# An exponential on VectorE in fewer steps, beside ScalarE's: attention and a Mish layer on one Trainium2 core

## The chip, the cores and the metric

The kernel runs on one core of one Trainium2 chip. The core has five engines that run their own instruction streams and meet at semaphores: TensorE (PE, matrix products into the PSUM banks), ScalarE (ACT), VectorE (DVE), GpSimd (POOL) and SyncE (SP, which here issues most of the DMAs). The metric is the time of one execution on the device in microseconds. The kernel before takes 830.16 us (median of three runs, 829.76 to 830.72).

## The reference, cut to what matters

`x` has 2048 tokens of 640 features in bf16. One branch is full softmax attention with 32 heads of 20 features. The other is a dense layer with 1536 hidden features and the Mish activation. A gate per token mixes the two.

```python
g = sigmoid((x * gate_w).sum(-1, keepdims=True))
qkv = (x @ wqkv).reshape(B, S, 3, 32, 20)            # to q, k, v per head
scores = einsum("bhqd,bhkd->bhqk", q, k) * 20 ** -0.5
a = einsum("bhqk,bhkd->bhqd", softmax(scores), v) ... @ wo
h = x @ w1 + b1
b = (h * tanh(softplus(h))) @ w2
return g * a + (1 - g) * b
```

The scores hold 32 x 2048 x 2048 values, and each needs an exponential. That is the bulk of the elementwise work.

## The kernel before, in words

**Tiling.** A *unit* is one head's scores for 128 keys against 512 queries: one PSUM bank of 128 x 512 floats. There are 2048 units. They are ordered in *groups* `(c, g)`: query block `c` of 512 queries, head group `g` of 4 heads, 16 key tiles. The order is all `g` with `c` = 0 and 1 first, then `c` = 2, then `c` = 3, whose last head group is cut into two halves of 256 queries. Three units make a *slot* (`compose`); there are 683 slots, and two sets of three PSUM banks take turns.

**One slot.** `emit_s` puts the three score products on TensorE (`score_mms`, L1149). Each uses 32 rows of the array, so the three run side by side. `emit_e` (L1171) puts one exponential over the slot on ScalarE, from PSUM to the tile `ETS` in bf16 (five slots deep, `NETS`). `emit_pv` and `pv` (L1456) then multiply V with the exponentials of four heads at a time. Four products side by side make one *pass* that accumulates into the bank `ACC`. V has a column of ones, so the sums of the softmax come out with it. After a group's last pass `group_done` copies the accumulator out (L1537) and divides.

**Units on VectorE.** For some slots `choose` takes a unit out of the order and gives it to VectorE as the third of the slot. Then ScalarE's instruction covers only two units (1024 columns a row instead of 1536). `emit_x` (L1216) evicts the third: scaled and biased, the float becomes an int16 whose bits, read as bf16, are 2^e times a linear mantissa. Four such units make a *batch*. When it is full (or `tight` says that its group ends soon), `close` queues the rest of its work on VectorE:

- `fraction` (L1287): the mantissa bits with the exponent of one, F, into the pad `u`
- `power` (L1283): the exponent bits alone, E, into the pad `E`
- `square` (L1291): F times F, to fp16, in place in `u`
- `cubes` (L1330): V scaled by a constant, into the tile `VC`, once per head group and key tile
- `times_f` (L1295): F squared times the evicted value, in `u`

The exponential is then a sum of three terms, and `emit_off` adds them by three passes on TensorE: the evicted value with V, E with V, and `u` with the scaled V. A *pad* is a tile of four units of bf16. Pads are borrowed from buffers that are not in use at the time (`open_pads`, `take_pad`, `give_pad`): parts of `QT`, `KT`, `OTN`, `HB`, `W2R`, `REG`, `PADS`.

**What sets the order.** The whole program is written out in Python before it runs. `Plan` keeps an estimated clock per engine (constants at the top: `EXP`, `QUAD`, `DOUBLE`, `CHAIN` and others) and puts each instruction where it fits by that clock. On VectorE, `work` picks among lanes: the division of a finished group (`norm`), the batches (`soon`, two lanes), Mish (`blend`) and others (`bg`). On TensorE, dense products (*tasks*: the projections, the hidden layer at L911, its second product at L970, the output at L994) are put into the gaps with due times (`pick`, `put`), and `fill_up` adds repeated or idle products where TensorE would rest too long. Whether a unit goes to VectorE is decided in `choose`, by VectorE's backlog (`BEHIND`, `crowded` with `IDLE`), by the distance to the group's end (`tight` with `CROWD` and `MARGIN`), by free pads, and by `room` for what VectorE still owes.

**The guard.** The bit form of the exponential holds only for a limited range of scores. `gram_task` bounds the scores from products of the weights and of `x` with themselves, `flag_ops` and `flag_end` compare the bound with `SAFE`, and if it is exceeded a second, safe program runs after the first.

Of the kernel before, what the change touches and what calls it, by code (L numbers as in the profile page):

```python
# [8 lines left out]
FP32 = mybir.dt.float32  # L9
BF16 = mybir.dt.bfloat16  # L10
I32 = mybir.dt.int32
I16 = mybir.dt.int16
# [24 lines left out]
NETS = 5  # L37
# [4 lines left out]
SAFE = 30.0  # L42
# [11 lines left out]
SPUN = 0.6  # L54
# [4 lines left out]
HALF_WORK = 0.60  # L59
LANES = 2  # L60
TAKEN = 3.6
LATE_OFF = 0.8
# [4 lines left out]
CHAIN = 4.4  # L67
FILL = 2.5
GIVE_BACK = 30
IDLE = 6  # L70
QUAD = 0.60
DOUBLE = 1.134
CUBES = 0.022
AHEAD = 14
SPREAD = 2
GAP = 0.8
SLOW_LOAD = 5.0
EARLY = 4
BEHIND = 7.0
PATIENCE = 3.0  # L80
CATCH_UP = 5.0
BUSY = 0.6
CROWD = 1.4
MARGIN = 0.5
EAGER = 30
# [6 lines left out]
LAG = 9  # L92
SPARE = 3.5
# [3 lines left out]
PACKED_Q = 12  # L97
# [7 lines left out]
REFILL = 0.58  # L105
# [15 lines left out]
MANTISSA = 0x7F  # L121
EXPONENT = 0x7F80
ONE = 0x3F80
# [110 lines left out]
def bass_gated_mix__softmax_full_mha__dense_activation_mish__prompt_kernel(  # L234
# [39 lines left out]
    VC = sb("VC", [P, NKT, HG, EW], BF16)  # L274
# [7 lines left out]
    MXR = OUTT[:, 48:56].bitcast(FP32)  # L282
    GW = OUTT[:, 64:64 + NFT]
# [93 lines left out]
    def attention(pl, fast):  # L377
# [133 lines left out]
        if fast:  # L511
# [29 lines left out]
            blank = OTN[0:NG, 0, 0:2, :].rearrange("p g t -> p (g t)")[:, 0:D]  # L541
            m_blank = pl.add("dve", lambda e: e.memset(blank, 0.0), cost=0.25)
# [282 lines left out]
            def gram_task(n, due):  # L825
# [3 lines left out]
                blocks = [(WQ, WK)[n] for _ in range(4)] if n < 2 else [WQ, WK] if n == 2 else [xt(n - 3)] * 4  # L829

                def mm(b, f):
                    at = 4 if n == 2 else b
                    block = blocks[b][:, f, at * P:(at + 1) * P]
                    return lambda e, bank: e.matmul(
                        PS[:, bank, b * P:(b + 1) * P], block, block, start=(f == 0), stop=(f == NFT - 1))

                def finish(bank, last):
                    for reads in ([wq_read], [wkv_read], [wq_read, wkv_read])[n] if n < 3 else [x_read[n - 3]]:
                        reads.append(last)
                    if n == 2:  # L840
                        to, src = MXS[:, 1:4:2], PS[:, bank, 0:2 * P].rearrange("p (a b) -> p a b", b=P)
                    else:
                        to, src = MXS[:, (0, 2, 0, 4, 5, 6, 7)[n]:][:, 0:1], PS[:, bank, :]
                    grams[n] = dve(lambda e: e.tensor_reduce(to, src, AX.X, ALU.max), [last], WIDE)
                    if len(grams) == 7:
                        bg.append((0.3, lambda: flag_ops(grams.values()), None))
                    return grams[n]

                return Task([mm(b, f) for b in range(len(blocks)) for f in range(NFT)], 0.06, finish, due,
# [236 lines left out]
        open_batch = [None]  # L1086
        batches = {}
        n_batches = [0]
        cubed = {"of": None, "tiles": set(), "read": None}
# [123 lines left out]
        def emit_x(s):  # L1213
# [8 lines left out]
            if len(batch["units"]) == BATCH:  # L1222
                close()
# [7 lines left out]
        def close():  # L1231
# [763 lines left out]
```

## Time and profile before

| | |
|---|---|
| median of 3 runs | 830.16 us (829.76 to 830.72) |
| the profiled execution's own time | 830.66 us |
| its span, first to last instruction | 828.8 us |
| ScalarE busy | 809.2 us, 98% |
| VectorE busy | 763.7 us, 92% |
| TensorE busy | 745.7 us, 90% |
| exponentials on ScalarE (L1171) | 683 instructions, 790.1 us |
| mean granted TensorE clock | 0.994 |
| DMA | 48.51 MB, 59 GB/s on average |

All times of the trace are of that one execution. "Busy" is the time in which an engine has at least one instruction in flight; instructions of one engine overlap a little, so the recorded durations add up to more. A row of a group gives the line, the engine, the operation, the tiles written and read, the shape, the count, then busy time and the mean duration in ns, and last the idle time ahead of it and what ended it. In a table of stretches, a row gives the window, its length, and for each engine the busy time with the number of instructions in brackets, then the granted clock, the DMA share and GB/s.

### The profile page before, as it was taken

To read this page: it belongs to the slowest core of one execution; us is meant where nothing else is said; L and a number is where in the kernel's file an instruction comes from. 1 tells how busy PE (TensorE), PEld (TensorE's weight loads), DVE (VectorE), ACT (ScalarE), POOL (GpSimd) and SP (SyncE) were. 2 spreads that over 40 slices of the span, in tenths; PEclk is the share of its full clock that TensorE was granted. 3 is DMA by queue.
4 is the path that set the end of the run, shared out by engine and by line. 5 is a ranking of instruction groups with operands and counts; after the bars stand their busy time and mean duration, and the time that the engine had idled before them with its cause. 6 is when DMAs were issued, how large, how long until landed. Compare 5 with 4: busy or idle time off the path is not lost.

```text
span 828.8 us, 16585 instructions
## 1 busy us (share of the span) xinstructions
PE 745.7 (90%) x6839; PEld 267.3 (32%) x6876; DVE 763.7 (92%) x1204; ACT 809.2 (98%) x714; POOL 7.3 (1%) x14
## 2 busy tenths in 40 slices
PE   8998988989888989889998998999889899999996
PEld 3333233233222333223333333333333333333332
DVE  4898878999999999988899899999999999999886
ACT  6999999999999999999999999999999999999995
POOL 3000000000000000000000000000000000000000
PEclk9999999999999999999999999999999999999998
DMA  9712210121123312141121221102121202100001
GB/s 228 94 52 76 66 59 11 50 72 57 47 59 97 113 47 60 54 118 40 37 72 34 59 62 49 50 15 58 58 70 46 78 15 64 51 22 23 23 19 37
DMA packets 78183, 48.51 MB, mean 59 GB/s; under 512 B 23964, under 2 KB 73748, under 8 KB 78052
## 3 DMA queue, kind: packets, MB, share of 16 engines
q1 hardware_dynamic: 75732, 46.87, 21.2%
q8 instruction: 57, 0.93, 0.5%
q10 hardware_dynamic: 2256, 0.47, 0.3%
q0 software_dynamic: 112, 0.01, 0.2%
q14 instruction: 26, 0.21, 0.1%
HBM read 37.64 MB, written 7.52 MB: 54 GB/s over the span
## 4 chain that ended last, share of the span: by engine, by line
ACT 91%; PE 5%; DVE 3%; issue 0%
ACT ETS L1171 88%; ACT REG L944 2%; PE PS L1149 1%; PE PS L1456 1%; ACT W2R L944 1%; PE PS L545 1%; PE PS L590 0%; PE PS L911 0%; PE PS L659 0%; DVE HB L1291 0%; DVE QT L1216 0%; PE PS L730 0%; DVE W2R L1216 0%; PE PS L765 0%; DVE HB L1000 0%
## 5 line engine op out<-in xcount | busy, mean ns | idle before, releaser
L1171 ACT ACTIVATE ETS<-PS 128x1024 bf16<-128x1024 f32 (+1 forms) x683 | 790.1, 1410 | 4.4 <-PE PS L1149 3.4
L1149 PE MATMUL PS<-QT,KT 32*128 32x512 bf16 (+1 forms) x2148 | 271.0, 378 | 66.1 <-ACT ETS L1171 48.4
L1456 PE MATMUL PS<-ETS,V_all 128*21 128x512 bf16 (+1 forms) x1783 | 191.2, 380 | 0.1
L1149 PEld LDWEIGHTS PS<-QT,KT 32*128 32x128 bf16 x2148 | 68.2, 91 | 270.9 <-ACT ETS L1171 234.2
L970 PE MATMUL PS<-W2R,HB 128*128 128x320 bf16 x384 | 72.8, 302 | 0.3 <-DVE XB L977 0.3
L1456 PEld LDWEIGHTS PS<-ETS,V_all 128*21 128x21 bf16 x1783 | 47.5, 90 | 76.6 <-issue 72.6
L1216 DVE TENSOR_SCALAR QT<-PS 128x512 int16<-128x512 f32 x76 | 52.0, 684 | 5.4 <-PE PS L1149 5.2
L911 PE MATMUL PS<-XB,REG 128*128 128x256 bf16 x360 | 55.4, 277 | 0.8 <-DVE HB L921 0.4
L1216 DVE TENSOR_SCALAR OTN<-PS 128x512 int16<-128x512 f32 x71 | 48.3, 680 | 2.0 <-PE PS L1149 1.8
L1216 DVE TENSOR_SCALAR PADS<-PS 128x512 int16<-128x512 f32 x61 | 41.6, 683 | 5.9 <-PE PS L1149 5.7
L970 PEld LDWEIGHTS PS<-W2R,HB 128*128 128x128 bf16 x384 | 29.3, 97 | 36.0 <-issue 26.0
L911 PEld LDWEIGHTS PS<-XB,REG 128*128 128x128 bf16 x360 | 28.9, 98 | 26.6 <-issue 24.1
L921 DVE TENSOR_TENSOR HB<-PS,B1T 128x512 bf16<-128x512 f32 x48 | 32.8, 684 | 3.2 <-PE PS L911 2.7
L1216 DVE TENSOR_SCALAR REG<-PS 128x512 int16<-128x512 f32 x35 | 23.9, 682 | 4.2 <-PE PS L1149 4.1
L1291 DVE TENSOR_TENSOR QT<-QT 128x1024 f16<-128x1024 bf16 (+2 forms) x35 | 25.0, 717 | 0.0
L994 PE MATMUL PS<-WOQ,QT 128*128 128x320 bf16 x128 | 24.3, 302 | 0.6 <-DVE QT L1530 0.5
L792 PE MATMUL PS<-REG,XB 128*128 128x160 bf16 (+1 forms) x240 | 23.4, 234 | 1.3 <-DVE WOQ L668 0.8
L994 PE MATMUL PS<-WOQ,OTN 128*128 128x320 bf16 x128 | 24.0, 302 | 0.1
L1216 DVE TENSOR_SCALAR KT<-PS 128x512 int16<-128x512 f32 x34 | 23.1, 681 | 0.6 <-PE PS L1149 0.6
L1537 DVE COPY OUNG<-PS 128x512 f32<-128x512 f32 x31 | 21.1, 682 | 1.6 <-PE PS L1456 1.4
L659 PE MATMUL PS<-XB,WOQ 128*128 128x512 bf16 x66 | 20.5, 383 | 1.9 <-issue 1.3
L944 ACT ACTIVATE REG<-HB 128x1024 f32<-128x1024 bf16 x18 | 22.2, 1236 | 0.0
(229 smaller groups left out, 900.2 us busy)
## 6 DMA issues: line engine op xcount, KB each, us to landing
REG<-in_B_w_dram SPq DMA_DIRECT2D x36, 320.0 KB, 3.1
BCT<-SUMS SPq DMA_DIRECT2D x124, 64.0 KB, 2.1
W2R<-in_B_w_dram SPq DMA_DIRECT2D x12, 320.0 KB, 3.3
KT<-KS SPq DMA_DIRECT2D x28, 128.0 KB
QT<-QS SPq DMA_DIRECT2D x112, 20.0 KB
QS<-WOQ SPq DMA_DIRECT2D x16, 128.0 KB, 1.7
KS<-OTN SPq DMA_DIRECT2D x16, 128.0 KB, 1.7
W2R<-in_B_w_dram SPq DMA_DIRECT2D x1, 1920.0 KB, 8.5
```

The costliest lines, as they stand in the source:

```text
L792: return lambda e, bank: e.matmul(PS[:, bank, i * n:(i + 1) * n], xt(t // 4)[:, f, t % 4 * P:(t % 4 + 1) * P], WV[:, f, g * HD:g * HD + n] ...
L911: return lambda e, bank: e.matmul(PS[:, bank, i * HW:(i + 1) * HW], w1b(n1)[:, f, i * P:(i + 1) * P], xt(c)[:, f, cols], start=(f == 0), s ...
L921: ev = dve(lambda e: e.tensor_tensor(hb, PS[:, bank, :].rearrange("p (i t) -> p i t", i=2), bias, ALU.add), [last, b_load, *guarded, *b_re ...
L944: ex = pl.add("act", lambda e: e.activation(U, h, AF.Tanh, scale=0.5, bias=-MISH_AT / 2), [ev, u_free[0]], cost=0.95)
L970: return lambda e, bank: e.matmul(PS[:, bank, 0:HALF], HB[:, hc % 2, f, t * P:(t + 1) * P], W2[:, f, half * HALF:(half + 1) * HALF], start ...
L994: return lambda e, bank: e.matmul(PS[:, bank, 0:HALF], otn(c, g, fast)[:, t * P:(t + 1) * P], WOG[:, g, half * HALF:(half + 1) * HALF], st ...
L1149: op = pl.add("pe", lambda e, i=i, g=real(g), tile=tile, j=j, cols=cols, c=c, of_q=of_q: e.matmul(scores(s)[:, i, cols], KT[32 * j:32 * j ...
L1171: e_op[s] = pl.add("act", lambda e: e.activation(ETS[:, s % NETS, 0:n, :], scores(s)[:, 0:n, :], AF.Exp, scale=SCALE, bias=LIFT if fast el ...
L1216: ev = dve_by(lambda e: e.tensor_scalar(block(batch["y"], n, I16), scores(s)[:, 2, :], SCALE * ULPS, BIAS, ALU.mult, ALU.add), [s_op[s], * ...
L1291: return lambda e: e.tensor_tensor(some_of(batch["u"], sp, FP16), some_of(batch["u"], sp, BF16), some_of(batch["u"], sp, BF16), ALU.mult)
L1456: lasts[n] = pl.add("pe", lambda e, v=v, j=j, src=src[:, cols], of_q=of_q, count=count: e.matmul(PS[32 * j:32 * j + EW, ACC, of_q], v, src ...
L1537: ev = dve(lambda e: e.tensor_copy(src, PS[:, ACC, :]), [last, oung_free[0]], WIDE)
```

## The change

The exponential on VectorE gets two terms in place of three. The eviction now makes an int16 whose bits are read as fp16 (10 bits of mantissa, 5 of exponent). `fraction` puts the mantissa under the exponent of one half. The product `times_y` multiplies that with the evicted value itself. `power` keeps the exponent bits, sets one low bit and works in place in the evicted pad. The two pads, read as fp16, are multiplied with the same bf16 V. The square, the scaled V (`VC`) and the third pad are gone. Since fp16 has a smaller range, `SAFE` goes from 30 to 9.75, and the guard bounds the weights by the row sums of absolute values within each head.

Two batches may be open at once. A pass with V is put out when two are ready, or when the oldest waiting unit is three slots old. `ETS` has six slots, and a number of the planner's constants are changed.

```diff
-NETS = 5
+NETS = 6
+OLD = 3
+WAITED = 3
+OWE = 0.6
-SAFE = 30.0
+SAFE = 9.75
-SPUN = 0.6
+SPUN = 0.65
-LATE_OFF = 0.8
+LATE_OFF = 0.5
-CHAIN = 4.4
+CHAIN = 3.3
-IDLE = 6
+IDLE = 5
+IDLE_2 = 4
+IDLE_3 = -1
+OPEN = 2
-GAP = 0.8
+GAP = 0.5
-BEHIND = 7.0
-PATIENCE = 3.0
+BEHIND = 8
+PATIENCE = 5
-CROWD = 1.4
-MARGIN = 0.5
-EAGER = 30
+CROWD = 1.6
+MARGIN = 2.5
+EAGER = 20
-LAG = 9
-SPARE = 3.5
+LAG = 25
+SPARE = 7
-PACKED_Q = 12
+PACKED_Q = 15
-REFILL = 0.58
+REFILL = 0.66
-ULPS = 128 / math.log(2)
-CUBE = 0.1669921875
-BIAS = 16113
-LIFT = (BIAS - 128 * (127 - 1.1157324)) * math.log(2) / 128
+ULPS = 1024 / math.log(2)
+BIAS = 15 * 1024 + 436
+LIFT = math.log(1.5069154) + 436 / ULPS
-MANTISSA = 0x7F
-EXPONENT = 0x7F80
-ONE = 0x3F80
+MANTISSA = 0x3FF
+EXPONENT = 0x7C00
+HALVES = 0x3800
+MORE = 8
...
-    VC = sb("VC", [P, NKT, HG, EW], BF16)
...
+                        got = dve(lambda e: e.tensor_reduce(
+                            sums, PS[0:w, bank, 0:heads * DH].rearrange("p (h d) -> p h d", d=DH), AX.X, ALU.add,
+                            apply_absolute_value=True), [last, m_mxs], WIDE)
...
             def reserve():
                 def run():
                     batch["u"], got["u"] = take_pad(batch)
-                    batch["E"], got["E"] = take_pad(batch)
...
+            def fraction(sp):
+                return lambda e: e.tensor_scalar(
+                    some_of(batch["u"], sp, I16), some_of(y, sp, I16), MANTISSA, HALVES, ALU.bitwise_and, ALU.bitwise_or)
+
+            def times_y(sp):
+                return lambda e: e.tensor_tensor(
+                    some_of(batch["u"], sp, FP16), some_of(batch["u"], sp, FP16), some_of(y, sp, FP16), ALU.mult)
+
             def power(sp):
                 return lambda e: e.tensor_scalar(
-                    some_of(batch["E"], sp, I16), some_of(y, sp, I16), EXPONENT, None, ALU.bitwise_and)
-            def square(sp):
-                return lambda e: e.tensor_tensor(
-                    some_of(batch["u"], sp, FP16), some_of(batch["u"], sp, BF16), some_of(batch["u"], sp, BF16), ALU.mult)
-            def times_f(sp):
-                return lambda e: e.tensor_tensor(
-                    some_of(batch["u"], sp, BF16), some_of(batch["u"], sp, FP16), some_of(y, sp, BF16), ALU.mult)
+                    some_of(y, sp, I16), some_of(y, sp, I16), EXPONENT, MORE, ALU.bitwise_and, ALU.bitwise_or)
...
             piece(QUAD, fraction, lambda: [*evs, *got["u"]], step("f"))
-            piece(QUAD, power, lambda: [*evs, *got["E"]], end_e)
-            piece(DOUBLE, square, lambda: [got["f"]], step("s"), True)
-            cubes()
-            piece(DOUBLE, times_f, lambda: [got["s"]], end, True)
+            piece(DOUBLE, times_y, lambda: [got["f"]], end, True)
+            piece(QUAD, power, lambda: [got["u"]], end_e)
...
             if s - 1 not in off:
                 return False
-            if open_batch[0]:
-                todo += len(open_batch[0]["units"]) * CHAIN / BATCH
+            todo += sum(len(b["units"]) for b in opened) * CHAIN / BATCH
             run = 1 + (s - 2 in off) * (1 + (s - 3 in off))
-            return todo >= (IDLE, IDLE - 2, -1)[run - 1]
+            return todo >= (IDLE, IDLE_2, IDLE_3)[run - 1]
...
+            def fits(group, taken):
+                mine = [v for v in near[2:] if v[:2] == group and v[3] not in taken and v[2] < tiles(*group) - 1]
+                return [v for v in mine if v[2] < 3] if near[2][:2] != group else mine
+
+            for batch in list(opened):
+                group = batch["group"]
+                mine = fits(group, js + [u[3] for u in batch["units"]])
+                if mine and len(batch["units"]) < BATCH:
+                    break
+                if not mine and near[2][:2] != group and place[near[2][:2]] > place[group]:
+                    close(batch)
+            else:
+                if len(opened) == OPEN:
+                    return None
                 group = near[2][:2]
...
-                if not free_pads() or len(open_pads()) - waiting - 1 < 2 or tiles(*group) < 4:
+                if not free_pads() or len(open_pads()) - waiting - 1 < 1 or tiles(*group) < 4:
...
-                for name in ("F", "E", "U"):
+                for name in ("U", "E"):
...
-                    home = batch[{"F": "y", "E": "E", "U": "u"}[name]]
-                    deps = batch["evs"] if name == "F" else [op]
-                    lasts = pv([(u, block(home, i), deps if i == 0 else []) for i, u in enumerate(batch["units"])], name == "U")
+                    home = batch["u" if name == "U" else "y"]
+                    lasts = pv([(u, block(home, i, FP16), [op] if i == 0 else []) for i, u in enumerate(batch["units"])])
...
-                emit_off((c, g), False, False, 1)
+                if passes > 50 or pl.now["pe"] + PASS + (SWITCH if pl.kind != "V" else 0) <= latest[0]:
+                    emit_off((c, g), False, False, 1)
...
-                if passes < 50 and queue[0][0] > step - 2 and pl.now["pe"] + PASS + (SWITCH if pl.kind != "V" else 0) > latest[0]:
+                if passes < 50 and queue[0][0] > step - OLD and pl.now["pe"] + PASS + (SWITCH if pl.kind != "V" else 0) > latest[0]:
...
-            emit_pv(step, 2 if step < NSLOT - 1 else 99)
-
-            while owed > 0:
+            turn = not fast or step >= NSLOT - 1 or pv_ready() >= 2 or bool(queue) and queue[0][0] <= step - WAITED
+            if turn:
+                emit_pv(step, 2 if step < NSLOT - 1 else 99)
+
+            while owed > (OWE if turn and fast and step < NSLOT else 0):
```

More of the change, by code (lines that the diff above doesn't have):

```diff
@@ L541, in attention @@
             blank = OTN[0:NG, 0, 0:2, :].rearrange("p g t -> p (g t)")[:, 0:D]
+            m_mxs = pl.add("dve", lambda e: e.memset(MXS, 0.0), cost=0.1)
             m_blank = pl.add("dve", lambda e: e.memset(blank, 0.0), cost=0.25)
@@ L1240, in close @@
             evs = list(batch["evs"])
-            batch["parts"]["F"] = evs[-1]
             got = {}
@@ L1298, in end @@
             def end(op):
-                batch["parts"]["U"] = op
-                batch["read"].append(op)
+                got["u"] = batch["parts"]["U"] = op
             def end_e(op):
                 batch["parts"]["E"] = op
-            def cubes():
-                of = real(group[1])
-                need = sorted({tile for u in batch["units"] for tile, _, _ in subs(*u[:3])})
-                def wait():
-                    if any((of, tile) not in v_done for tile in need):
-                        return False
-                    if cubed["of"] == of:
-                        return None
-                    if any("U" not in b["begun"] for at in groups[:place[group]] for b in batches.get(at, ())):
-                        return False
-                    return cubed["read"]
-                def run():
-                    deps = []
-                    if cubed["of"] != of:
-                        deps.append(cubed["read"])
-                        cubed.update(of=of, tiles=set())
-                    if all(tile in cubed["tiles"] for tile in need):
-                        return
-                    t0, t1 = min(tile for tile in range(NKT) if tile not in cubed["tiles"]), need[-1] + 1
-                    while t1 < NKT and (of, t1) in v_done and safe(v_done[(of, t1)]) <= pl.now["dve"]:
-                        t1 += 1
-                    cubed["tiles"].update(range(t0, t1))
-                    pl.add("dve", lambda e: e.tensor_scalar(
-                        VC[:, t0:t1, :, :].rearrange("p t h d -> p t (h d)"),
-                        V_all[:, t0:t1, of * HG:(of + 1) * HG, :].rearrange("p t h d -> p t (h d)"), CUBE, None, ALU.mult),
-                        [*deps, *(v_done[(of, tile)] for tile in range(t0, t1))], cost=0.08 + (t1 - t0) * CUBES)
-                lane.append((0.3, run, wait, due))
@@ L1412, in emit_off @@
             for batch in batches.get(group, []) if fast else []:
-                if open_batch[0] is batch and last and not any(v[:2] == group for v in islice(order, 80)):
-                    close()
-                for name in ("F", "E", "U"):
+                if batch in opened and last and not any(v[:2] == group for v in islice(order, 80)):
+                    close(batch)
+                for name in ("U", "E"):
                     if name in batch["begun"]:
```

97 lines of the change are left out of this document (40 added, 57 removed).

## The prediction

> **What bounds the kernel now.** I read first the table of busy time by stretch, then ScalarE's groups by shape, then the chain of waits in order of time, then VectorE's lines one by one, and last who waits for whom. The stretches (length, then busy time and instructions of PE, PE's weight loads, VectorE, ScalarE, GpSimd; granted clock, DMA share, GB/s):
>
> ```profile
> 40.00:800.00 760.00, 690.29 (x6238) 244.41 (x6272) 717.93 (x1120) 756.33 (x668) 0.00 (x0) 1.00 0.19 54
> ...
> 80.00:120.00 40.00, 36.17 (x340) 13.59 (x341) 30.67 (x52) 40.00 (x36) 0.00 (x0) 1.00 0.20 61
> ...
> 360.00:400.00 40.00, 36.55 (x337) 11.62 (x333) 35.43 (x57) 40.00 (x37) 0.00 (x0) 1.00 0.14 33
> ...
> 520.00:560.00 40.00, 36.63 (x324) 12.58 (x321) 39.70 (x61) 40.00 (x37) 0.00 (x0) 1.00 0.11 32
> ...
> 760.00:800.00 40.00, 38.23 (x365) 13.04 (x361) 33.84 (x57) 40.00 (x36) 0.00 (x0) 1.00 0.06 17
> ```
>
> Between 40 and 800 us ScalarE is busy for 756.33 of 760 us: it sets the end. VectorE is at 717.93, or 94.5%, and in stretches such as 520 to 560 it is full (39.70 of 40). The idle 42.07 us lie in stretches such as 80 to 120 and 760 to 800. ScalarE's exponentials, by shape (busy, mean ns of one):
>
> ```profile
> L1171 ACT ACTIVATE ETS<-PS 128x1536 bf16<-128x1536 f32 x363 | 549.7, 1612 | 2.9 <-PE PS L1149 2.0 <-PE PS L1456 0.8
> L1171 ACT ACTIVATE ETS<-PS 128x1024 bf16<-128x1024 f32 x320 | 357.7, 1182 | 1.5 <-PE PS L1149 1.5
> ```
>
> There are 683 slots of three score blocks. In 320 of them VectorE takes the third block. A slot so relieved is 1.612 - 1.182 = **0.430 us** shorter. The durations overlap in the pipe: the page gives 790.1 us for all 683, so a whole slot costs (790.1 + 320 x 0.430) / 683 = 1.358 us and a relieved one 0.928. Hence the number of relieved slots is what sets the time, and what limits that number, in most stretches, is VectorE.
>
> **The price of a block on VectorE.** The same chain of waits, where it runs through VectorE (start, length):
>
> ```profile
> 61.38 0.60 DVE W2R L1216
> 61.98 0.60 DVE HB L1291
> ...
> 66.22 1.13 DVE HB L1295
> ...
> 117.97 0.69 DVE PADS L1287
> 118.67 0.60 DVE KT L1283
> ```
>
> Back to back, a step is shorter than its recorded duration by some 0.08 us: 0.60 for an eviction recorded at 0.68, and 1.13 for a product over four blocks against these records:
>
> ```profile
> L1291 DVE TENSOR_TENSOR PADS<-PADS 128x2048 f16<-128x2048 bf16 x8 | 9.7, 1217 | 0.0
> ...
> L1295 DVE TENSOR_TENSOR OTN<-OTN 128x2048 bf16<-128x2048 f16 x6 | 7.3, 1215 | 0.0
> ```
>
> Each line of the offload over the whole span; the rows are, in this order, the eviction L1216, the fraction L1287, the power L1283, the square L1291, the product L1295 and the scaled V L1330:
>
> ```profile
> 0.00:829.00 829.00, 217.31 (x319) 0.99 0.22 59
> ...
> 0.00:829.00 829.00, 55.49 (x88) 0.99 0.22 59
> ...
> 0.00:829.00 829.00, 55.17 (x88) 0.99 0.22 59
> ...
> 0.00:829.00 829.00, 104.64 (x136) 0.99 0.22 59
> ...
> 0.00:829.00 829.00, 103.52 (x129) 0.99 0.22 59
> ...
> 0.00:829.00 829.00, 12.00 (x26) 0.99 0.22 59
> ```
>
> **The change, part by part.**
>
> *Removed from VectorE:* the square and the scaled V, 104.64 + 12.00 = 116.64 us as recorded; less 162 x 0.08 for the overlap, **103.7 us**, or 0.324 us for each of 320 blocks.
>
> *Kept on VectorE:* eviction, fraction, one product, power: 217.31 + 55.49 + 55.17 + 103.52 = 431.49, less 624 x 0.08 = 381.6, or **1.192 us a block** (from the chain, 0.60 + (0.69 + 0.60 + 1.13) / 4 = 1.205: the same). The product now has two fp16 inputs and an fp16 result. The two rows above have one fp16 side each and the same duration, so I take no change; the bounds are 1.13 and, if it fell to the pace of the 512-column float eviction (0.60 a block), 2.40 a batch. The power gets a second bit operation; the fraction has two already and costs 0.69 against 0.60, so +0.00 to +0.09 a batch, and I take 0.
>
> *The sum.* If VectorE stays at its 94.5%, what was removed is spent on d further blocks, while every block shortens the span, and so VectorE's time, by 0.430 x 0.945 = 0.406: d = 103.7 / (1.192 + 0.406) = **65**. That is 385 relieved slots, and 65 x 0.430 = **28.0 us**. From the profiled execution's 830.66 us (span 828.8 and 1.86 outside it; 0.06% over the median of 830.16) this gives **802.7 us**. The bounds of this one unknown, how much of the freed time is spent, are d = 0 and the case in which the idle 42.07 us are filled to 1% as well: 34.5 us more, (103.7 + 34.5) / 1.598 = 86 blocks, 37.0 us, 793.7. I take 65, since the stretches that are full outnumber the others; on the loose ones see the rivals.
>
> *TensorE.* A batch had three extra passes with V and has two. The passes follow each other at 0.22 us; a pass after scores comes 0.32 after them, so a change of kind costs some 0.10 (start, length):
>
> ```profile
> 442.84 0.10 PEld L1149 LDWEIGHTS PS<-QT,KT 32*128 32x128 bf16 x3 [0.28 <-ACT ETS L1171]
> 442.85 0.39 PE L1149 MATMUL PS<-QT,KT 32*128 32x512 bf16 x3
> 443.16 0.10 PEld L1456 LDWEIGHTS PS<-REG,VC 128*21 128x21 bf16 x4 [0.23 <-issue]
> 443.17 0.40 PE L1456 MATMUL PS<-REG,VC 128*21 128x512 bf16 x4
> ...
> 443.39 0.39 PE L1456 MATMUL PS<-ETS,V_all 128*21 128x512 bf16 x4
> ```
>
> 88 batches x 3 become 106 x 2: 52 passes or 11 us less. Passes in pairs save between 0 (already paired) and 0.10 x 362 = 36 us (724 passes, each second change of kind gone); half is 18. So TensorE's 690.29 us become some 661 over 732, the 90% of now: it neither helps nor takes over. The cover for its work is its wait for ScalarE, which in turn hardly ever waits for it:
>
> ```profile
> PE PS L1149 <- ACT ETS L1171: 48.4, 140, 1.0
> ...
> ACT ETS L1171 <- PE PS L1149: 3.4, 8, 0.8
> ```
>
> Without that cover every late pass would cost its 0.22 us. The moving operand of the passes becomes fp16 beside a bf16 V; the trace has no such matmul. Bounds: 0.22 a pass as for bf16, and 0.43, which the slow stretch quoted below shows (697.23 - 696.80); 212 x 0.21 = 45 us of TensorE at worst. I take 0.22.
>
> *Waits.* A pass may now stay back until a second one is ready or three slots have gone by. In the instruction stream that is order, not a semaphore; the scores of the next slot stand behind the pair. What stays occupied longer is a slot of ETS, and there are six in place of five. The power writes over its own input and so waits for the product; the E passes come later by one product (1.13), and behind them the last pass of the group and the copy of the accumulator at L1537. A batch's chain after its last eviction is nevertheless shorter: 2.42 us where it was 0.69 + 0.60 + 2 x 1.13 = 3.55.
>
> *Pads.* A batch holds two pads where it held three, and two batches may be open. That costs no instruction; it is what could fill the loose stretches.
>
> *Guard.* The weights' Gram tasks go from 50 matmuls of 128 columns to 80 of 80, 6400 columns in both; three small reductions and a memset are new. The nearest small row is the reciprocal at 0.24 us: about 1 us of VectorE, worth 0.3 us of time, neglected. No DMA is added, moved or removed, and no issue passes another on a queue. From the reference's own inputs the largest row sums within heads are 3.25 and 3.14 and the largest squared norm of a token 1.90, so the exponent is bounded by sqrt(3.25 x 3.14) x 1.90 / sqrt(20) = 1.36 against 9.75: the second, safe program is not entered.
>
> *Planner constants.* Between 760 and 800 us VectorE idles for 6 us though ScalarE is full: there a rule limits the blocks, not time. The rules move both ways: a second relieved slot in a row is refused from 5 us of backlog instead of 6, and all open blocks count; a batch near its group's end needs 2.5 us of margin instead of 0.5; but a batch of the next group can open beside the old one.
>
> **The rivals.**
>
> *More: the loose stretches fill too* (793.7, above). For it: pads, and 9.3 us of idle VectorE at 80 to 120. Against it: the tighter margins.
>
> *Less: the rules bind first.* If half of the freed time is spent, d = 32 and the time is 816.9; VectorE would then fall to about 87%. For it: at 760 to 800 room was left unused already. Against it: 520 to 560, where 0.3 us was left.
>
> *It does not do what it says:* the number of blocks stays at 320 and VectorE only idles, 830.7. Against it stand all the full stretches.
>
> *Slower: the pair comes ahead of the scores.* In a relieved slot TensorE has 0.93 us for the scores (0.32), a pair (0.22 + 0.32) and its share of the dense work. If the pair goes first, the scores and so ScalarE are late by one pass, 0.22. There are 724 / 2 = 362 pairs, 385 of 683 slots are relieved, so 204 pairs meet one: all late is 45 us, 802.7 + 45 = 848. It decides from 28.0 / 45 = 62% of them on. Against it: only 8 waits, 3.4 us, in the whole of before.
>
> *Slower: the clock.* Around 696 us the granted clock falls and a pass takes 0.64 in place of 0.39:
>
> ```profile
> 680.00:700.00 20.00, 18.19 (x152) 7.07 (x150) 19.43 (x29) 19.83 (x18) 0.00 (x0) 0.91 0.18 50
> 700.00:720.00 20.00, 18.97 (x167) 7.43 (x168) 18.95 (x27) 19.62 (x18) 0.00 (x0) 1.00 0.20 56
> ...
> 696.80 0.64 PE L1456 MATMUL PS<-ETS,V_all 128*21 128x512 bf16 x2
> ...
> 697.23 0.64 PE L1456 MATMUL PS<-OTN,V_all 128*21 128x512 bf16 x2
> ```
>
> ScalarE lost 0.17 + 0.38 = 0.55 us in those 40. To eat 28 us it would take 51 such drops; there is one in the middle of this trace. The Trainium skill, "TensorE: Matmul & The Clock Gate", section "What's actually happening", has the clock halve after an idle window of about 3.4 us, and work taken off TensorE and bundled into pairs goes that way. By that rule a drop could follow whenever TensorE rests; the trace agrees that drops exist, with one in 760 us.
>
> *FP16 at half pace:* 45 us of TensorE against 48.4 of cover, which lies in 140 places and not where the passes are; with a third uncovered, 802.7 + 15 = 818. The Trainium skill, "FP8 and Floating Point Precision", section "TensorE Precision Notes", puts bf16 and fp16 through the same widening before the multiply, which would give 802.7; no run here shows it.
>
> **How the numbers follow.** The forecast, 797 to 810 around **803 us**, gets 0.56; more, 0.12; less (half pace among it), 0.18; no change 0.04; slower 0.10 (the pair 0.07, the clock 0.03). The range that leaves out some 2 in 10 is 791 to 823: it holds the forecast and most of the two cases beside it. 0.2% (1.7 us) is what a measurement can tell here from no change. Faster 0.86, same 0.04, slower 0.10.
>
> **What would show it.** Right: some 385 exponentials of 1024 columns and 298 of 1536, still 0.43 apart; about 762 us busy at L1171; no VC group; product and power at 1.22 and 0.68 as recorded; VectorE still near 94% between 40 us and the start of the last 29; ScalarE's wait for scores under 10 us. Wrong: 340 relieved slots and VectorE under 90% (less); a wait of ScalarE for L1149 of tens of us (the pair); passes from the fp16 pads at 0.43 us spacing; a granted clock below 0.97.

## The result, and the profile after

The changed kernel takes **800.4 us** (median; 800.19 to 800.83) against 830.44 in the same comparison: a ratio of 0.9638, 95% interval 0.9621 to 0.9654, or 30.0 us less. The profiled execution took 800.83 us with a span of 799.0.

First the stretch from 40 us to the last 29 us, of the kernel before and of the changed kernel (columns as before: length; PE, PE's weight loads, VectorE, ScalarE, GpSimd busy; granted clock, DMA share, GB/s), then the exponentials of the changed kernel by shape:

```profile
40.00:799.80 759.80, 690.09 (x6230) 244.23 (x6260) 717.73 (x1120) 756.13 (x668) 0.00 (x0) 1.00 0.19 54
...
40.00:770.00 730.00, 668.41 (x6038) 238.23 (x6037) 697.49 (x1116) 729.39 (x668) 0.00 (x0) 1.00 0.21 56
```

```profile
L1185 ACT ACTIVATE ETS<-PS 128x1536 bf16<-128x1536 f32 x303 | 496.4, 1694 | 1.1 <-PE PS L1163 1.1
L1185 ACT ACTIVATE ETS<-PS 128x1024 bf16<-128x1024 f32 x380 | 438.8, 1268 | 1.0 <-PE PS L1163 1.0
```

There are 380 relieved slots where there were 320. The two shapes lie 1694 - 1268 = 426 ns apart. All 683 exponentials together were 790.09 us busy and are 764.59 (row below, first), 25.5 us less: 60 x 0.425. The span fell by 29.8, so 4.3 us came from elsewhere. ScalarE idled for 3.67 of 759.8 us in this stretch before, and now for 0.61 of 730. Over the whole span its idle time fell by 2.6 us (from 19.6 to 17.0), and its work other than the exponentials by 1.7 (from 19.1 to 17.4): these are the 4.3.

VectorE is busy for 95.5% of the stretch (94.5% before). Its lines of the offload over the whole span of the changed kernel; the rows are, after that of the exponentials, the eviction L1230, the fraction L1294, the product L1298 and the power L1302:

```profile
0.00:840.00 840.00, 764.59 (x683) 1.00 0.23 58
...
0.00:840.00 840.00, 258.24 (x379) 1.00 0.23 58
...
0.00:840.00 840.00, 66.75 (x116) 1.00 0.23 58
...
0.00:840.00 840.00, 123.88 (x162) 1.00 0.23 58
...
0.00:840.00 840.00, 67.22 (x116) 1.00 0.23 58
```

Together 516.09 us in 773 instructions; less 0.08 each, as the prediction took it off, 454.2 us or 1.195 us a block.

TensorE with an fp16 moving operand: the group of passes from one kind of pad, then two passes that follow each other, an fp16 one and a bf16 one (start, length), then the two waits between TensorE and ScalarE.

```profile
L1422 PE MATMUL PS<-QT,V_all 128*21 128x512 f16 x179 | 20.4, 384 | 0.2 <-DVE OUNG L1504 0.2
```

```profile
448.66 0.40 PE L1422 MATMUL PS<-QT,V_all 128*21 128x512 f16 x4
...
448.88 0.60 PE L1422 MATMUL PS<-ETS,V_all 128*21 128x512 bf16 x6
```

```profile
PE PS L1163 <- ACT ETS L1185: 51.2, 152, 1.0
...
ACT ETS L1185 <- PE PS L1163: 2.1, 5, 0.6
```

The fp16 pass lasts 384 ns as the bf16 one did, and the next follows at 0.22 us. ScalarE waits for scores for 2.1 us in all.

### The profile page after: what moved, and what is told of

It reads as the page before. It is cut to its first block, busy times and chain, and to the rows that moved or that the text cites. A ratio compares the mean times of both kernels' runs of the same rounds, so it can differ in the third digit from the quotient of the medians.

```text
span 799.0 us, 16266 instructions
## 1 busy us (share of the span) xinstructions
PE 722.8 (90%) x6665; PEld 261.2 (33%) x6665; DVE 739.9 (93%) x1195; ACT 782.0 (98%) x714; POOL 7.3 (1%) x14
## 4 chain that ended last, share of the span: by engine, by line
ACT 94%; PE 2%; DMA 2%; SPq 1%; DVE 1%; issue 0%
ACT ETS L1185 91%; ACT REG L959 2%; DMA XB<-in_A_x_dram 2%; SPq L531 1%; ACT W2R L959 1%; PE PS L1163 1%; PE PS L1422 0%; PE PS L798 0%; PE PS L596 0%; DVE HB L1015 0%; SPq L558 0%; PE PS L1009 0%; DVE KT L1230 0%; SPq L525 0%; DVE HB L936 0%
## 5 line engine op out<-in xcount | busy, mean ns | idle before, releaser
L1185 ACT ACTIVATE ETS<-PS 128x1024 bf16<-128x1024 f32 (+1 forms) x683 | 764.6, 1457 | 2.1 <-PE PS L1163 2.1
L1422 PE MATMUL PS<-ETS,V_all 128*21 128x512 bf16 (+1 forms) x1722 | 166.9, 375 | 0.0
L985 PE MATMUL PS<-W2R,HB 128*128 128x320 bf16 x384 | 69.4, 302 | 1.1 <-DVE XB L992 0.9
L1230 DVE TENSOR_SCALAR QT<-PS 128x512 int16<-128x512 f32 x87 | 59.6, 685 | 9.1 <-PE PS L1163 8.2
L1422 PEld LDWEIGHTS PS<-ETS,V_all 128*21 128x21 bf16 x1722 | 42.5, 90 | 43.1 <-issue 29.4
L1230 DVE TENSOR_SCALAR PADS<-PS 128x512 int16<-128x512 f32 x79 | 53.8, 685 | 2.8 <-PE PS L1163 2.6
L1230 DVE TENSOR_SCALAR OTN<-PS 128x512 int16<-128x512 f32 x77 | 52.4, 681 | 2.2 <-PE PS L1163 2.1
L985 PEld LDWEIGHTS PS<-W2R,HB 128*128 128x128 bf16 x384 | 30.2, 97 | 34.3 <-issue 20.4
L1230 DVE TENSOR_SCALAR KT<-PS 128x512 int16<-128x512 f32 x46 | 31.3, 685 | 4.1 <-PE PS L1163 4.0
L1230 DVE TENSOR_SCALAR REG<-PS 128x512 int16<-128x512 f32 x40 | 27.2, 683 | 0.8 <-PE PS L1163 0.6
L1702 PE MATMUL PS<-KT 128*128 128x512 bf16 x82 | 24.8, 384 | 0.0
L665 PE MATMUL PS<-XB,REG 128*128 128x512 bf16 x80 | 23.4, 384 | 0.0
```

The source lines that it names most:

```text
L665: return lambda e, bank: e.matmul(PS[:, bank, :], W[:, f, base:base + P], xt(c)[:, f, :], start=(f == 0), stop=(f == NFT - 1))
L985: return lambda e, bank: e.matmul(PS[:, bank, 0:HALF], HB[:, hc % 2, f, t * P:(t + 1) * P], W2[:, f, half * HALF:(half + 1) * HALF], start ...
L1185: e_op[s] = pl.add("act", lambda e: e.activation(ETS[:, s % NETS, 0:n, :], scores(s)[:, 0:n, :], AF.Exp, scale=SCALE, bias=LIFT if fast el ...
L1230: ev = dve_by(lambda e: e.tensor_scalar(block(batch["y"], n, I16), scores(s)[:, 2, :], SCALE * ULPS, BIAS, ALU.mult, ALU.add), [s_op[s], * ...
L1422: lasts[n] = pl.add("pe", lambda e, v=v, j=j, src=src[:, cols], of_q=of_q, count=count: e.matmul(PS[32 * j:32 * j + EW, ACC, of_q], v, src ...
L1702: pl.add("pe", lambda e: e.matmul(PS[:, bank, :], k[:, 0:P], k, start=True, stop=True), [free], cost=PASS, kind="S")
```

## The experiments

Each took one part of the change away, or did one part alone. One table holds all of them. *Exponentials* is the busy time of that line, *rest* is the span less it. VectorE's share and ScalarE's idle time are for the stretch from 40 us to the last 29. These columns come from one profiled execution; the time is the median of several, and each ratio is against the kernel before in the same session (medians of 830.4 to 830.9).

| kernel | relieved slots | exponentials, us | rest, us | VectorE | ScalarE idle, us | time, us | ratio (95%) |
|---|---|---|---|---|---|---|---|
| before | 320 | 790.1 | 38.7 | 94.5% | 3.7 | 830.4 | 1 |
| changed | 380 | 764.6 | 34.4 | 95.5% | 0.6 | 800.4 | 0.9638 (0.9621 to 0.9654) |
| e1 arithmetic alone | 344 | 780.5 | 45.6 | 86.9% | 7.7 | 826.5 | 0.9941 (0.9925 to 0.9958) |
| e2 square put back | 334 | 784.3 | 44.5 | 97.4% | 0.2 | 829.1 | 0.9975 (0.9963 to 0.9988) |
| e3 one open batch | 357 | 775.1 | 37.2 | 90.6% | 0.7 | 814.2 | 0.9802 (0.9785 to 0.9818) |
| e4 no pairs | 366 | 771.3 | 36.5 | 92.2% | 2.6 | 809.4 | 0.9737 (0.9721 to 0.9753) |
| e5 arithmetic, two open | 366 | 771.1 | 55.4 | 90.1% | 16.0 | 825.5 | 0.9927 (0.9907 to 0.9947) |
| e6 all but constants | 369 | 769.6 | 55.7 | 90.7% | 14.0 | 825.6 | 0.9943 (0.9924 to 0.9962) |
| e7 no filling | 375 | 766.3 | 37.7 | 93.7% | 3.1 | 807.3 | 0.9726 (0.9705 to 0.9748) |
| e8 unseen work | 372 | 774.1 | 60.0 | 96.8% | 17.0 | 836.2 | 1.0074 (1.0055 to 1.0093) |
| e9 filling alone | 369 | 769.6 | 53.9 | 90.9% | 12.6 | 828.2 | 0.9967 (0.9957 to 0.9976) |
| e10 old timing rules | 370 | 768.0 | 40.8 | 93.3% | 3.1 | 810.2 | 0.9755 (0.974 to 0.977) |
| e11 old load rules | 356 | 775.8 | 43.6 | 88.8% | 8.8 | 820.7 | 0.9877 (0.9862 to 0.9892) |
| e12 more relieved | 384 | 762.8 | 34.3 | 96.2% | 0.7 | 799.0 | 0.9623 (0.961 to 0.9636) |

Two things are to be read from it at once. The exponentials lie on one line in all kernels but e8: 790.1 less 0.425 us for each relieved slot beyond 320, within 1.0 us. So the price of a slot, 0.425 us, holds in thirteen of the fourteen kernels. The rest, however, runs from 34 to 60 us, and that is where most of these kernels lost what the slots had gained.

**e1: the arithmetic alone.** The kernel before with the new fraction, product, power and guard, two pads a batch, and nothing of the new order:

```diff
-CHAIN = 4.4
+CHAIN = 3.3
+            piece(DOUBLE, times_y, lambda: [got["f"]], end, True)
+            piece(QUAD, power, lambda: [got["u"]], end_e)
...
 NETS = 5, IDLE = 6, MARGIN = 0.5, ... as before; one open batch; no pairs
```

> The kernel before with the new two-term exponential and its guard alone: one open batch, no pairing, five ETS slots and all planner constants as before, except the estimated work of a batch (4.4 to 3.3 us). The program holds some 344 relieved slots, 24 more than before and 36 fewer than the changed kernel. Theory (each relieved slot is worth 0.43 us and VectorE's freed time is worth only what the order written out makes of it): 830.4 - 24 x 0.43 = 820 us, VectorE's busy share between 40 us and the last 29 us falls to some 86 to 88%, ScalarE's waits for scores stay under 10 us. Rival (VectorE's time is what counts and is spent by itself): within 3 us of 800. Rival (pairs and the other order matter to TensorE): ScalarE's waits grow and the time lies well off the 0.43 line.

```profile
40.00:797.10 757.10, 690.27 (x6017) 242.51 (x6018) 658.24 (x1042) 749.43 (x669) 0.00 (x0) 0.98 0.20 54
```

```profile
ACT ETS L1180 <- PE PS L1158: 7.0, 14, 1.3
ACT PADS L1818 <- PE PS L1004: 4.9, 1, 4.9
```

The count, 24 more slots, and VectorE's 86.9% came as the first theory had them. Most of the freed time simply lies idle (98.9 us of VectorE in the middle, 42.1 before), which rules out that cheaper arithmetic is spent by itself. But the time is 826.5 and not 820: the rest grew by 6.9 us, with ScalarE idle for 7.7 us in the middle. Of these, 5.6 us lie in stretches in which the granted clock fell (330 to 340, 430 to 460, 500 to 520 and 740 to 750 us).

**e2: the new order with the old price.** The changed kernel with one more product a batch, which the planner knows of as an instruction; the estimate that its load rules use for a whole batch (`CHAIN`) stays at 3.3:

```diff
+            def extra(sp):
+                return lambda e: e.tensor_tensor(
+                    some_of(batch["u"], sp, FP16), some_of(y, sp, FP16), some_of(y, sp, FP16), ALU.mult)
+            piece(DOUBLE, extra, lambda: [*evs, *got["u"]], step("x"), True)
-            piece(QUAD, fraction, lambda: [*evs, *got["u"]], step("f"))
+            piece(QUAD, fraction, lambda: [got["x"]], step("f"))
```

> The changed kernel with one more product over four blocks per batch on VectorE (its result is overwritten, the output is the same), known to the planner. All the new order is there, and VectorE's price per block is back near the old one (1.48 us). The program holds some 334 relieved slots. Theory: 800.4 + 46 x 0.43 = 820 us, with VectorE again near 93 to 95% in the middle. Rival (the new order and not the cheaper exponential brought the gain): the time stays under 808. Rival (TensorE's third pass was what cost): under 808 as well, since TensorE's passes stay at two a batch.

```profile
40.00:799.80 759.80, 684.99 (x6183) 243.16 (x6183) 740.42 (x1167) 759.62 (x677) 0.00 (x0) 1.00 0.19 54
799.80:828.80 29.00, 15.40 (x163) 5.97 (x157) 15.93 (x37) 9.73 (x9) 0.86 (x1) 0.67 0.09 26
```

```profile
ACT PADS L1834 <- PE PS L1009: 12.4, 1, 12.4
```

```profile
812.59 1.03 DVE L1298 TENSOR_TENSOR REG<-REG,OTN 128x1024 f16<-128x1024 f16 x2
813.67 0.61 PE L1427 MATMUL PS<-REG,V_all 128*21 128x256 f16 x6 [2.98 <-DVE REG L1298]
```

Here VectorE is full (97.4%) and ScalarE hardly starves (0.2 us). The exponentials fall to 784.3 us, as the slots say. The 10 us missing against the 820 expected are in the last 29 us: ScalarE is busy for 9.7 of them (20.7 in the changed kernel) and waits 12.4 us for the last products. The last exponential ends at 809.0 us, and the last batch's product on VectorE only at 813.6; TensorE stands waiting for it for 2.98 us (the rows just above), and its granted clock is 0.67 in this stretch. Whether a `CHAIN` that fits the dearer batch would have closed it in time was not tried. With the square back almost the whole gain is gone, so neither half of the change carries it: the cheap arithmetic alone is worth some 4 us, the new order with the dear arithmetic some 2 us, both together 30. Without the loss in the last stretch the new order alone would be worth some 9 us (5.8 of exponentials and 3.5 of ScalarE's idle time in the middle), which is still far from 30.

**e3 and e4: one open batch; no pairs.**

```diff
-OPEN = 2
+OPEN = 1
```

> The changed kernel with one batch open at a time in place of two. The program holds some 357 relieved slots, 23 fewer. Theory: 800.4 + 23 x 0.43 = 810 us, VectorE's share in the middle lower by some 3 points. Rival (the second open batch only shifts work): within 2 us of 800.

```diff
-            turn = not fast or step >= NSLOT - 1 or pv_ready() >= 2 or bool(queue) and queue[0][0] <= step - WAITED
+            turn = True
-OWE = 0.6
+OWE = 0.0
```

> The changed kernel with the passes with V put out at each slot as before, without waiting for a second one, and without the debt that the dense work may carry over (OWE 0). The program holds some 366 relieved slots, 14 fewer. Theory: 800.4 + 14 x 0.43 = 806 us; the bursts of passes on TensorE are shorter and more changes of kind stand in its stream. Rival (pairing itself delays the scores): without pairs the time is at or under 800 in spite of fewer relieved slots. Rival (pairs matter to TensorE beyond the count): over 812, with ScalarE waiting for L1163 by 10 us or more.

e3 costs 13.8 us, of which 10.5 are the slots; VectorE falls to 90.6% and ScalarE idles no more than in the changed kernel. So with these constants the second batch is what keeps VectorE supplied with blocks. e4, without the pairs and without the debt of the dense work, costs 9.0 us, 6.7 of them the slots and some 2 in idle time of ScalarE. Pairs do not delay the scores (the first rival, since the time is not under 800) and are only to a small part a matter of stalls (the second, since it is not over 812); they go with a higher count.

**e5 and e6: the change built up from e1.** e5 adds the two open batches, e6 also the pairs. What e6 lacks is thirteen of the planner's constants, nothing else.

```diff
+OPEN = 2          # e5 and e6, with fits() and the loop over opened
+NETS = 6          # e6, with OLD and OWE
+turn = ... pv_ready() >= 2 ...
 IDLE = 6, BEHIND = 7.0, CROWD = 1.4, MARGIN = 0.5, LATE_OFF = 0.8, GAP = 0.8, REFILL = 0.58, SPUN = 0.6,
 PATIENCE = 3.0, LAG = 9, SPARE = 3.5, EAGER = 30, PACKED_Q = 12 as before
```

> The kernel before with the two-term exponential (as in e1) and, of the new order, only the two open batches with their way of choosing a unit; no pairing, five ETS slots, planner constants as before. The program holds some 366 relieved slots, 22 more than e1. Theory (what e1 lacked was a second open batch, so that freed VectorE time could be spent): exponentials 764.6 + 14 x 0.425 = 770.5 us, and with the 36 to 39 us of the rest of the changed kernel or of the kernel before 807 to 810 us. Rival (without pairs TensorE cannot follow the shorter slots): the rest is 45 us or more as in e1, ScalarE waits for scores for over 7 us, the granted clock is near 0.98, and the time is 815 or more.

> As e5, with the pairing of passes (and six ETS slots and the debt of the dense work) as well; what is missing of the change is the planner's constants. The program holds some 369 relieved slots. Theory: 764.6 + 11 x 0.425 = 769.3 us of exponentials and a rest of 35 to 38: 804 to 807 us. Rival (the constants hold the gain): 812 or more. Against e5 it says what pairs are worth: the difference beyond 0.425 us for each slot is theirs.

Both theories on the time were too hopeful, and both rivals have the times. The slots are there (366 and 369, exponentials at 771.1 and 769.6 us as expected), and yet the times are 825.5 and 825.6. The rest is 21 us larger than in the changed kernel; in e6, 13.4 of it is idle time of ScalarE in the middle, and in the last 29 us ScalarE is busy for 5.0 less. The reason that e5's rival gave, missing pairs, falls with e6: the pairs are there and the time is the same, so with the constants as before pairs are worth nothing that these runs show. In e5 the chain that ended last is no longer ScalarE's alone, and in e6 VectorE and TensorE wait for each other (who waits for whom; us, times, longest):

```profile
ACT 70%; PE 13%; DVE 12%; DMA 2%; SPq 2%; issue 1%; ACTq 0%; DVEq 0%
```

```profile
DVE OTN L1231 <- PE PS L1164: 8.9, 9, 3.2
DVE KT L1231 <- PE PS L1164: 8.4, 8, 2.3
...
PE PS L1164 <- DVE OTN L1231: 5.1, 11, 1.8
...
ACT ETS L1186 <- PE PS L1164: 11.6, 20, 2.0
```

One of the places in e6 in order of time (start, length, in brackets the idle time ahead and what ended it):

```profile
68.53 0.69 DVE L1303 TENSOR_SCALAR KT<-KT 128x2048 int16<-128x2048 int16 x1
68.76 0.39 PE L1164 MATMUL PS<-QT,KT 32*128 32x512 bf16 x3 [0.68 <-DVE PADS L1231]
...
69.20 1.94 ACT L1186 ACTIVATE ETS<-PS 128x1024 bf16<-128x1024 f32 x2 [0.29 <-PE PS L1164]
...
70.94 0.59 PE L666 MATMUL PS<-XB,WOQ 128*128 128x512 bf16 x1 [0.96 <-DVE V_all L780]
72.04 0.61 PE L1164 MATMUL PS<-QT,KT 32*128 32x512 bf16 x3 [0.51 <-DMA KT<-KS]
...
72.69 1.45 ACT L1186 ACTIVATE ETS<-PS 128x1536 bf16<-128x1536 f32 x1 [1.55 <-PE PS L1164]
```

The scores wait 0.68 us for an eviction that VectorE does late, and ScalarE starves for 0.29. TensorE then waits 0.96 us for VectorE once more, and at 71.0 us the granted clock falls; after a further wait of 0.51 for keys from the DMA, a score product takes 0.61 us at 72.04 where it took 0.39 at 68.76, and ScalarE starves for 1.55. The stretch just before the drop and the drop itself:

```profile
67.60:71.00 3.40, 1.76 (x27) 1.01 (x25) 3.29 (x6) 3.11 (x3) 0.00 (x0) 1.00 0.22 70
71.00:77.60 6.60, 6.09 (x30) 1.21 (x30) 2.52 (x5) 3.54 (x4) 0.00 (x0) 0.50 0.27 85
```

At half the clock ScalarE is busy for 3.54 of 6.60 us. So this one drop goes with a loss of 3.1 us, where the prediction put 0.55 on a drop.

**e7 and e9: the clock.** e7 takes out of the changed kernel the products that `fill_up` adds; e9 puts the change's constant for them into e6. `emit_s` adds idle products of its own by another constant (`GAP`), and these stay in both.

```diff
-SPUN = 0.65       # e7
-STREAM = 0.48
+SPUN = 0.0
+STREAM = 0.0
...
-SPUN = 0.6        # e9, in e6
+SPUN = 0.65
```

> The changed kernel without the repeated and idle products that fill TensorE's pauses (SPUN and STREAM 0). The program holds some 375 relieved slots. Theory if the clock does not matter here: 800.4 + 5 x 0.425 = 802.5 us. Rival (the clock gate, as the prediction put it, 0.55 us for each drop): the granted clock falls under 0.97, ScalarE waits for scores for 10 us or more, and the time is over 808.

> As e6 (everything but the constants, 825.6 us), with one constant of the change, SPUN 0.65 in place of 0.60: repeated or idle products are put in until 65% of a window on TensorE is planned as busy. 369 relieved slots as in e6. In e6 the granted clock fell in three places between 40 and 780 us, and ScalarE idled for 5.0 us in those stretches and for 9.1 in others. Theory A (the drops of the clock are a good part of e6's stalls): the drops are gone, 818 to 821 us. Theory B (the stalls come from the order of VectorE's and TensorE's work): the time stays within 3 us of e6. If the change's other constants were only decoration: 804.

e7 lies between its two theories: 807.3 us, with ScalarE idle for 2.5 us more and 5 slots fewer. But 62 of the 82 idle products are still there (the changed kernel has 82), so that it is no test without filling. In its trace the granted clock stays at 0.996 on average, so no clock of under 0.97 explains it. Over its four executions the time goes with the clock (805.9 us at 0.996, 806.3 at 0.995, 808.4 and 809.5 at 0.993).

```profile
L1702 PE MATMUL PS<-KT 128*128 128x512 bf16 x62 | 20.3, 386 | 0.0
```

The three stretches of e6 in which the clock fell (columns as in the first table of stretches):

```profile
60.00:80.00 20.00, 17.54 (x163) 5.97 (x162) 13.66 (x23) 16.16 (x15) 0.00 (x0) 0.83 0.17 52
...
200.00:220.00 20.00, 16.89 (x162) 5.83 (x159) 19.20 (x35) 19.46 (x19) 0.00 (x0) 0.94 0.09 26
220.00:240.00 20.00, 17.39 (x158) 6.27 (x156) 14.67 (x26) 19.40 (x18) 0.00 (x0) 0.97 0.21 62
```

In the traced execution of e9 one is left, at another place, but the time did not get better (828.2 against 825.6): ScalarE waits as before for the same things.

```profile
360.00:380.00 20.00, 18.26 (x158) 5.90 (x157) 16.44 (x28) 18.88 (x19) 0.00 (x0) 0.91 0.16 36
```

```profile
ACT ETS L1186 <- PE PS L1164: 10.5, 21, 2.0
...
ACT ETS L1186 <- PE PS L1423: 4.8, 2, 3.5
```

The time fits theory B, but e9 cannot decide between the theories, since its edit did not do what it was meant to. Of the idle products (products, then weight loads, in the middle of e6 and of e9; some products are missing in a trace) it adds ten, and none of them comes before 339 us, while the drops of e6 lie at 71 us and between 210 and 230:

```profile
40.00:796.30 756.30, 14.05 (x45) 3.14 (x45) 0.99 0.20 55
...
40.00:794.50 754.50, 14.14 (x47) 3.81 (x55) 1.00 0.20 55
```

Nor was the clock higher: it is 0.987 on average over e9's ten executions and 0.990 over e6's five. The traced execution of e9 is the one with the highest clock and the shortest time (825.4 us at 0.992; the longest is 829.9 at 0.981), and e6 behaves alike (824.9 at 0.992, 828.6 at 0.987). So drops go with lost time, and what they cost by themselves stays open. What the runs do show is that they are not most of it: of e6's 14.0 us of idle ScalarE 9.0 lie outside the three stretches, and e11 (below) idles for 8.8 us with a clock of 0.998 to 0.999 in every execution. In the place shown above (71 us in e6) the drop came behind waits for VectorE.

The Trainium skill, "TensorE: Matmul & The Clock Gate", section "What's actually happening", says that the clock is halved after at least one idle window of some 3.4 us. The trace of e6 agrees that it is halved (1.00 to 0.50 at 71.0 us), but shows no such pause ahead of it: in the 3.4 us before, TensorE was busy for 1.76 us, and its longest pause was 0.96.

**e8: work on VectorE that the planner doesn't see.** One more bit operation a batch, planned at no cost:

```diff
...
+            piece(0.0, extra, lambda: [*evs, *got["u"]], step("x"))
-            piece(QUAD, fraction, lambda: [*evs, *got["u"]], step("f"))
+            piece(QUAD, fraction, lambda: [got["x"]], step("f"))
```

> The changed kernel with one more bit operation over four blocks per batch on VectorE (0.60 us back to back, overwritten, the output is the same), which the planner takes for free. About 95 x 0.60 = 57 us more on VectorE; the program holds some 372 relieved slots (exponentials 768 us). VectorE had 32.5 us idle in the middle 730 us. Theory (VectorE is as much the bound as ScalarE): at least 57 - 32.5 = 24 us appear, 825 us or more, with VectorE over 97% busy and ScalarE waiting. Rival (VectorE's work has slack in time, ScalarE alone sets the end): under 808.

```profile
DVE 75%; PE 11%; ACT 10%; issue 2%; DMA 1%; SPq 0%; DVEq 0%
```

It costs 35.8 us, more than the 24 that VectorE's idle time could not hold. VectorE carries 75% of the chain where ScalarE carried 94%; it is 96.8% busy, just under the 97 expected. So the rival is out: in the changed kernel VectorE has no slack for work that the order was not written for. 8 relieved slots fewer and late evictions are part of the 35.8, and were not priced apart.

**e10 and e11: which constants.** The changed kernel with five constants of TensorE's timing as before, and with eight rules of VectorE's load as before:

```diff
+GAP = 0.8, REFILL = 0.58, SPUN = 0.6, EAGER = 30, PACKED_Q = 12                                # e10
+IDLE = 6, BEHIND = 7.0, CROWD = 1.4, MARGIN = 0.5, LATE_OFF = 0.8, PATIENCE = 3.0, LAG = 9, SPARE = 3.5   # e11
```

> The changed kernel with the five constants of TensorE's timing as before (GAP, REFILL, SPUN, EAGER, PACKED_Q), the rules of VectorE's load new. 370 relieved slots. Theory (TensorE's timing is what keeps ScalarE fed): 769 us of exponentials and a rest of 42 us or more, 812 us or more, with drops of the granted clock. Rival (VectorE's load rules do it): a rest of 36 to 38, 805 to 808.

> The changed kernel with the eight constants of VectorE's load as before (IDLE, BEHIND, CROWD, MARGIN, LATE_OFF, PATIENCE, LAG, SPARE), TensorE's timing new. 356 relieved slots. Theory (the load rules set the number of relieved slots, and hardly the stalls): 774.8 us of exponentials and a rest of 35 to 38, 811 to 814 us. Rival (they set the stalls too): a rest of 44 or more, 820 us or more.

```profile
ACT ETS L1185 <- PE PS L1163: 7.2, 13, 1.9
...
ACT ETS L1185 <- PE PS L1422: 2.5, 1, 2.5
```

The rows are e11's waits of ScalarE. For e11 the rival is the nearer one: 820.7 us and a rest of 43.6, with 8.8 us of ScalarE idle. The load rules set the count and also the stalls. e10 lies between its theories: 810.2 us, a rest of 40.8. Which of the eight rules matters was not tried. A different constant makes the planner write a different order from the first place at which it bites, so a single constant's worth could only be told from many orders. The same holds, to a lesser degree, for e3, e4, e7 and e10: each is one order, how much orders scatter was not measured, and a few us of each difference may be the luck of that order.

**e12: four more slots.**

```diff
-CROWD = 1.6
-BEHIND = 8
+CROWD = 1.7
+BEHIND = 8.5
```

> The changed kernel with CROWD 1.7 and BEHIND 8.5 in place of 1.6 and 8. 384 relieved slots, 4 more. Theory: 762.9 us of exponentials, 800.4 - 1.7 = 798.7 us. Rival (VectorE is full, so further blocks come back as stalls): 800.5 or more.

799.0 us, 1.4 less in the median, and the exponentials fell by 1.8 us for 4 slots. The intervals of the two ratios overlap, so that e12 is faster than the changed kernel is likely and not shown.

## Why the prediction was right, point by point

*The forecast of 802.7 (803) against 800.4.* Predicted were 65 slots of 0.430 us, 28.0 us. Measured were 60 slots of 0.425, 25.5 us, and 4.3 us of span from terms that the sum had at zero: ScalarE's own waits (2.6) and its other work (1.7). The two misses, 2.5 and 4.3, have opposite signs, so that it came as near as 2.3 us is luck.

*The slot's price.* 0.430 from the two mean durations; 0.425 from the busy times, within 1.0 us in thirteen of fourteen kernels. Right.

*The block's price on VectorE.* 1.192 forecast, 1.195 measured, both with 0.08 us taken off each instruction (more on this below). The product with two fp16 inputs kept its pace, and so did the power with two operations (both lie within that sum).

*"VectorE is what limits the number, so what is freed is spent."* This step was only half right, and it is the one that the experiments were needed for. With the new price and the old order (e1) 24 slots come and VectorE falls to 86.9%: the rival "less" is what the arithmetic by itself does. The step holds for the new order, where VectorE stood at 95.5% with the cheap price and at 97.4% with the dear one (e2). The prediction put the loose stretches down to pads and rules and did not ask what the freed time needs in order to be used: a second open batch (13.8 us when it is taken out) and the rules of the load (20.3 us). e1, e5 and e6 have the same cheap exponential and take 825 to 827 us, so the step did not follow from what the prediction gave for it. That the new rules spend nearly all that is freed was assumed, and there the forecast was lucky.

*"Planner constants: the rules move both ways."* Too little was made of them. Taken together they are the difference between 825.6 (e6) and 800.4, and they work by the rest more than by the count: 11 slots, 5 us, against 21 us of rest.

*TensorE.* "Neither helps nor takes over" was right: 91.6% busy in the middle (668.41 of 730) for a forecast of 90%. Some of that is filling: 82 idle products in place of 33 (by their weight loads; the trace has 26 of the 33 products).

*The slower rivals.* ScalarE's wait for scores went from 3.4 to 2.1 us, so the pair did not come ahead of the scores. The granted clock was 0.997 and fell nowhere in the middle; the 0.55 us put on a drop was too little for the one in e6 (3.1 us). FP16 runs at the pace of bf16 (384 ns against 385, next pass after 0.22 us).

*The guard* kept the second program out, as the bound of 1.36 had said: the 683 exponentials in the trace are those of one program.

*VectorE's busy time* is 739.9 us where 763.7 - 103.7 + 60 x 1.195 gives 731.7. The 8 us more are not further work: added up instruction by instruction, the lines of the offload fell by 29.2 us (550.0 to 520.8) and all others rose by 1.2 (297.6 to 298.8, the guard's reductions among them). A further 4.3 us were lost because neighbouring instructions overlap less (84.0 us of overlap before, 79.7 after): 29.2 - 1.2 - 4.3 = 23.7, and the busy time fell by 23.8. The prediction's 0.08 us off each instruction holds where the next one does not need its result. In the old order the power stood between the fraction and the square that needs it; the new chain is fraction, product, power, each of which needs the one before, and where two of them meet on VectorE there is as a rule no overlap (start, length, of the changed kernel):

```profile
430.54 0.68 DVE L1294 TENSOR_SCALAR REG<-QT 128x2048 int16<-128x2048 int16 x1
431.26 0.69 DVE L1298 TENSOR_TENSOR REG<-REG,QT 128x1024 f16<-128x1024 f16 x1
431.87 0.68 DVE L1230 TENSOR_SCALAR QT<-PS 128x512 int16<-128x512 f32 x1
432.47 0.68 DVE L1298 TENSOR_TENSOR REG<-REG,QT 128x1024 f16<-128x1024 f16 x1
433.19 0.69 DVE L1302 TENSOR_SCALAR QT<-QT 128x2048 int16<-128x2048 int16 x1
```

The product follows its fraction after 0.72 us and the power its product after 0.72, while the eviction between them, which needs neither, follows after 0.61. The instructions that begin with no overlap are 211 where they were 162. At 1.598 us a block, 8.2 us are about the five slots that were missing; that they are the reason was not tested.

What stays open: which of the rules makes the order stall less, and what a drop of the clock costs by itself.

## What to carry to other kernels

Work taken off a full engine is worth only what the order can put in its place: before it is counted as spent, look for what would have to be ready for it (here a block to evict, at the right moment, from a batch that may be open). Parts of such a change don't add up. Taken out one at a time the square's price, the second batch, the pairs and the two groups of rules cost 28.7, 13.8, 9.0, 20.3 and 9.8 us, 82 us out of a gain of 30, so an edit that shows nothing by itself may still be needed. Where two engines are both near full (here 99.9% and 95.5%), price the count (slots) and the stalls (rest) apart: the first followed one line in thirteen of the fourteen kernels, and the second decided.

## What the runs showed of the hardware that was not expected

A pass with a bf16 stationary and an fp16 moving operand takes what a bf16 pass takes (384 ns against 385, 0.22 us to the next).

On VectorE a step that needs the result of the one just ahead begins some 0.04 us after that one's recorded end, and one that doesn't begins some 0.08 before it (0.72 and 0.61 us from start to start in the rows above, for records of 0.68 and 0.69). That is 0.11 to 0.12 us a step, which an instruction put between the two that needs neither would save.

The recorded duration of one exponential rose from 1612 to 1694 ns and from 1182 to 1268 in the changed kernel, and fell to 1482 and 1060 in e8, while the busy time stayed on its line in the changed kernel. Over the fourteen kernels the 1536-column one is longest where ScalarE idled least (1704 ns in e2, 0.2 us idle) and shortest where it idled most (1482 in e8, 17.0 us). That would fit a record that includes time spent behind the instruction before; it was not tested. The difference of the two shapes (430, 426, 422 ns) is what held as a price.
